# A transformer block on one core: the opening stage in another order

## The chip, the cores and the metric

The kernel runs on one core of a Trainium2 chip. The metric is device time in microseconds (us). A core has a matrix engine (PE), a vector engine (DVE), an engine for activations and copies (ACT), a general engine (POOL) and a queue engine (SP) that here only starts transfers. Each engine works through its own instructions in program order and waits on semaphores of the others.

## The reference

One pre-norm block for 2048 tokens of width 448. `x` is 2048x448, there are 16 heads of 28, one key and one value head for all of them, and a gated feed-forward part of width 1792.

```
q = (ln(x) @ wq).reshape(B, S, 16, 28).transpose(0, 2, 1, 3)
k, v = ln(x) @ wk, ln(x) @ wv
p = softmax(einsum("bhqd,bkd->bhqk", q, k) * 28 ** -0.5)
h = x + einsum("bhqk,bkd->bhqd", p, v) @ wo          # heads put side by side
out = h + (silu(ln(h) @ w1) * (ln(h) @ w3)) @ w2
```

## The kernel before, in words

**Numbers in two parts.** Every operand of a large product is split into a high part of reduced precision and a low part, the rest. A product takes the terms high-high, low-high and high-low. So whoever makes an operand makes two: ACT copies the high part (`xh`, `WQ[0]`, `WKV[0]`), DVE or POOL subtracts it (`xl` on DVE, `WQ[1]` and `WKV[1]` on POOL).

**Quarters.** The tokens are worked in four quarters of 512 (`t` = 0 to 3), each a tile `X[t]` of 128x4x448, that is 896 KB. The trace calls all four X, the order of instructions calls them X_77 to X_80. The heads are worked in four groups (`g`).

**The opening stage** (lines 389 to 575) makes keys and values for all quarters and the queries `QR[t][:, g]`. In it, for each quarter, stand these steps:

- `stats(t)`: on DVE four statistics (L178, L179) and one addition (L183), then on POOL a power that gives the reciprocal deviation `rs` (L184).
- `norm(t)`: four scalings of `X[t]` into `xn` on DVE (L189), each followed by a small copy on POOL (L191).
- `tr(t)`: sixteen transposes on PE (L203) into four banks of the matrix memory, four copies `xh` on ACT (L211), four subtractions `xl` on DVE (L221, L223).
- `kv(t)`: eleven matmuls on PE (L150). ACT copies the keys (L473) and values (L475), SP starts a transfer that doubles the keys (L476), and after each second quarter POOL forms the difference `kd` of two quarters' keys (L478). `k_low(t)` subtracts on DVE (L483).
- `va(t)`: four small transposes of the values (L490) and a copy on DVE (L491).
- `q(t, g)`: eleven matmuls on PE (L150, operand OS, which is `WQ`) and a copy of the result by ACT (L502). For the first one, `build_qs(0)` makes the split query instead (L238 on ACT, L239 on DVE); `build_qs(1)` and `build_qs(2)` do this from `QR`.

**Units.** Between them stand quads, which find the largest score of each row for the softmax. They go in pairs. The first quad of a pair is four matmuls against `kd` (L257) and four `relu` copies on ACT (L267); the second is four matmuls against the keys (L257) and four operations on DVE (L271, called "both" here) that add the `relu` to the score and take the maximum. The `relu` copies of the next pair go into the same buffers, so they wait for "both" of this pair. Q1 to Q20 are the quads in the order in which they come; odd ones are against `kd`.

**Banks.** There are eight banks. `bank()` takes the one that was given back longest ago in program order, `done()` gives one back. A matmul into a bank waits for the reader of what stood there. So the order of the code alone fixes which reader each step of PE waits for.

**Transfers.** Each transfer started by SP or ACT signals on one of eight semaphores (lanes) that are dealt out in turn. A transfer on a lane is started only when the transfer before it on that lane has landed. Until then the engine that is to start it waits, with all that stands behind it in its queue. At the start these transfers come: `X[0]` in four pieces, the small weights of keys and values (`wkv`: three transfers for `wk`, three for `wv`, all started by ACT), `WQ` (three transfers into OT: 672, 112 and 112 KB), and `X[1]` to `X[3]`.

**Behind the opening stage** comes the attention loop (lines 629 to 663), whose first score matmul (L308) stands directly behind the last `q`, and then the feed-forward part. PE goes through all of it in one fixed order.

Of the kernel before, what the change touches and what calls it, by code (L numbers as in the profile page):

```python
# [40 lines left out]
def block_kernel(  # L41
# [13 lines left out]
    ve, se, ge, pe, sy = nc.vector, nc.scalar, nc.gpsimd, nc.tensor, nc.sync  # L55
    xv = x[0].rearrange("(t p n) d -> t p n d", t=NT, p=P, n=NQ)
# [3 lines left out]
    def f(ap):  # L60
        return ap.bitcast(F32)
# [4 lines left out]
    ln_pool = ctx.enter_context(tc.tile_pool(name="ln", bufs=2))  # L66
# [68 lines left out]
    def done(ps):  # L135
        free.append(used.pop(id(ps))[1])
# [2 lines left out]

    def mm_D(ps, lhs, rhs, lsl, rsl, between=None, part=False):


        terms = []
        for a, b in ((0, 0), (1, 0), (0, 1)):
            terms += [(a, c, b, c) for c in range(3)]
        terms += [(0, 3, 0, 3), (0, 3, 1, 3)][: 2 - part]
        for k, (a, ca, b, cb) in enumerate(terms):
            pe.matmul(  # L150
                ps, lhs[b][:, cb, lsl], rhs[a][:, ca, rsl],
                start=(k == 0), stop=(k == len(terms) - 1 and not part),
            )
            if between is not None and k == 5:
                between()

    def load_w(dst, w, eng=sy):
        eng.dma_start(dst[:, 0:3], w[0:384].rearrange("(c p) m -> p c m", p=P))
        eng.dma_start(dst[0:64, 3], w[384:448])
        eng.dma_start(dst[64:128, 3], w[384:448])  # L160
# [9 lines left out]
    LN = {}  # L170

    def ln_stats(t, n):
        if n == 0:
            LN[t] = (ln_pool.tile([P, NQ, 6], F32, name="st", bufs=NT),
                     ln_pool.tile([P, NQ, 2], F32, name="mv", bufs=NT),
                     ln_pool.tile([P, NQ], F32, name="rs", bufs=NT), {})
        st, mv, _, _ = LN[t]
        ve.bn_stats(st[:, n], X[t][:, n])  # L178
        ve.bn_aggr(mv[:, n], st[:, n])  # L179

    def ln_rstd(t, n0=0, n1=NQ):
        _, mv, rs, _ = LN[t]
        ve.tensor_scalar(rs[:, n0:n1], mv[:, n0:n1, 1], EPS, None, op0=ALU.add)  # L183
        ge.tensor_tensor(rs[:, n0:n1], rs[:, n0:n1], pexp[:, n0:n1], op=ALU.pow)  # L184

    def ln_norm(t, n, spare=False):
        _, mv, rs, xns = LN[t]
        xn = xns[n] = ln_pool.tile([P, 512], F32, name="xn", bufs=4)
        (ge if spare else ve).tensor_scalar(xn[:, :D], X[t][:, n], mv[:, n, 0:1], rs[:, n : n + 1],  # L189
                                            op0=ALU.subtract, op1=ALU.mult)  # L190
# [208 lines left out]
    def wkv(tl, k):  # L399
        return tl[:, k, :384].rearrange("p (c m) -> p c m", c=4)  # L400
# [2 lines left out]
    wkv_r, WKV = wkv(slot(7, F32, "wkv"), 0), slot(6, F32R, "wkvs")  # L403
    WKV = [wkv(WKV, k) for k in range(2)]
    ve.memset(wkv_r, 0.0)
    for m0, w in ((0, wk), (64, wv)):
        load_w(wkv_r[:, :, m0 : m0 + DH], w, se)
    load_w(wq_r, wq)
    for t in range(1, NT):
        sy.dma_start(X[t], xv[t])  # L410
    kb = keep.tile([64, 1], F32, name="kb")
    ge.tensor_tensor(kb, ident[:64, 28:29], ident[:64, 60:61], op=ALU.add)
    for k in range(2):
        ve.memset(f(WQ[k][:, :, :, DH:]), 0.0)
    se.activation(NGT[0][:, :P // 4], ident[:, :P // 4], AF.Copy)
    warm = bank()

    def heat(n):
        for _ in range(n):
            pe.transpose(warm[:, :P], ident, ident)  # L420
# [14 lines left out]
    def low_wq(c0, c1, eng):  # L435
        for c in range(c0, c1 + 1):
            eng.tensor_tensor(WQ[1][:, c, :, :DH], wq4[:, c], f(WQ[0][:, c, :, :DH]), op=ALU.subtract)

    def split_wq(c0, c1, eng=None):
        for c in range(c0, c1 + 1):  # L440
            se.activation(WQ[0][:, c, :, :DH], wq4[:, c], AF.Copy)
            if eng:
                low_wq(c, c, eng)
# [11 lines left out]
    def stats(t, *ns):  # L455
        for n in ns:
            ln_stats(t, n)
        if NQ - 1 in ns:
            ln_rstd(t)

    def norm(t):
        for n in range(NQ):
            ln_norm(t, n)

    def tr(t, *cs):
        for c in cs or range(4):
            ln_tr(t, c)
# [13 lines left out]
    def k_low(t, ps):  # L481
        cols = slice(t * T, (t + 1) * T)
        ve.scalar_tensor_tensor(KL[0:64, cols], ps[0:64], kb, f(KH[0:64, cols]), op0=ALU.add, op1=ALU.subtract)  # L483
        sy.dma_start(f(KL[64:128, cols]), f(KL[0:64, cols]))
        done(ps)

    def va(t, vt):
        ps = bank()
        for n in range(NQ):
            pe.transpose(ps[:, 32 * n : 32 * n + 32], vt[64:96, n * P : (n + 1) * P], ident[64:96, 64:96])  # L490
        ve.tensor_copy(VA[:, NQ * t : NQ * t + NQ, :DH],  # L491
                       ps[:, :P].rearrange("p (n r) -> p n r", n=NQ)[:, :, :DH])
        done(ps)

    def q(t, g, between=None):
        ps = bank()
        mm_D(ps, [w[:, :, 4 * g : 4 * g + 4].rearrange("p c h r -> p c (h r)") for w in WQ],
             XT[t], slice(0, P), slice(0, T), between)
        if t == g == 0:
            build_qs(0, ps)  # L500
        else:
            se.activation(QR[t][:, g], ps, AF.Copy)  # L502
        done(ps)
# [6 lines left out]
    def quads(n=1):  # L510
        while n > 0 and first:
            fn, *args = first.pop(0)
            fn(*args)
            n -= fn is quad
# [5 lines left out]
            ln_norm(0, n - 1)  # L520
    ln_norm(0, NQ - 1)
    split_wkv()
    split_wq(0, 3)
    ln_tr(0, 0, between=lambda: heat(8))
    done(warm)
    tr(0, 1, 2, 3)
    low_wq(0, 3, ge)
    v0, p0 = kv(0)
    stats(1, 0, 1, 2, 3)
    q(0, 0)  # L530
    k_low(0, p0)
    norm(1)
    q(0, 1)
    tr(1)
    v1, p1 = kv(1)
    stats(2, 0, 1, 2, 3)
    q(0, 2)
    k_low(1, p1)
    norm(2)
    q(0, 3)  # L540
    va(0, v0)
    va(1, v1)
    build_qs(1)
# [4 lines left out]
    stats(3, 0, 1, 2, 3)
    q(1, 0, quads)
    k_low(2, p2)  # L550
    norm(3)
    quads()
    q(1, 1, quads)
    va(2, v2)
    quads()
    q(1, 2, quads)
    q(1, 3)
    build_qs(2)
    quads()
    tr(3)  # L560
    quads()
    v3, p3 = kv(3)
    load_wo()
    q(2, 0)
# [15 lines left out]
    def at(s, fn, *args):  # L580
        todo.setdefault(s, []).append((fn, args))
# [8 lines left out]
    LAST = NC * NI  # L590
# [9 lines left out]
            at(e + 14 + 2 * n, ln_stats, t, n)  # L600
        at(e + 22, ln_rstd, t)
    for n in range(NQ):
        at(LAST - 24 + n, ln_norm, 0, n, True)
    for c in range(4):
        at(LAST - 17.5 + 4 * c, lambda c: ln_tr(0, c, True, True), c)
    for t in range(NT):
# [195 lines left out]
```

## Time and profile before

| | |
|---|---|
| median of 3 runs | 1195.22 us (1195.06 to 1196.54) |
| the profiled execution | 1196.01 us, span 1194.2 us |
| busy: PE, DVE, ACT, POOL | 1178.6, 811.2, 724.0, 332.4 us |
| mean granted clock of PE | 0.998 |
| opening stage, up to the first score matmul | 92.75 us of the span |

The span is the time from the first to the last instruction on the core; all times below count from its start. A row of the timeline has the start, the time from the first start to the last end of the merged instructions, the engine, the line, the operation, what it writes and reads, how many there are, and in brackets how long the engine sat idle before it and what ended that. ACTq and SPq are the queue sides of ACT and SP that start transfers. Successive instructions of one engine overlap a little, so what a step costs in a row of equal ones is read from start to start.

### The profile page before, as it was taken

The numbers are of one execution on the slowest core, as the hardware profiler recorded it, in microseconds if no ns is written. First come the engines' busy times: TensorE is split into PE (matmuls) and PEld (weight loads), VectorE is DVE, ScalarE is ACT, GpSimd is POOL, SyncE is SP. The second block draws the span as 40 slices with busy tenths as digits, with TensorE's granted clock in tenths as the row PEclk, the third lists the DMA queues.
The fourth block names the chain that finished last, engine by engine and source line by source line (L and its number), as shares of the span: only waits on it lengthen the run. The fifth ranks groups of instructions, "written<-read, shape, count | busy, mean of one in ns | idle before, by whom it ended". The sixth has DMA issues, their size and how long they took to land. (4 is left out here: it accounts for less than half of the span.)

```text
span 1194.2 us, 24111 instructions
## 1 busy us (share of the span) xinstructions
PE 1178.6 (99%) x9594; PEld 728.6 (61%) x9594; DVE 811.2 (68%) x1486; ACT 724.0 (61%) x1377; POOL 332.4 (28%) x256
## 2 busy tenths in 40 slices
PE   8999999999999999999999999999999999999998
PEld 6664444445544445444445443688888888888886
DVE  6758999998899997899997982254444445444333
ACT  3568999997799996899996999411211111111111
POOL 4211011101101110110110132363555455445552
PEclk9999999999999999999999999999999999999999
DMA  5010001000001000010000010114000000000000
GB/s 167 19 37 2 27 10 46 11 12 2 11 4 44 12 12 2 11 47 5 8 12 10 2 46 11 40 45 117 1 32 1 1 1 31 1 1 32 1 1 32
DMA packets 32377, 26.92 MB, mean 23 GB/s; under 512 B 10824, under 2 KB 28936, under 8 KB 32264
## 3 DMA queue, kind: packets, MB, share of 16 engines
q1 hardware_dynamic: 31144, 25.27, 7.2%
q8 instruction: 75, 1.23, 0.4%
q14 instruction: 38, 0.31, 0.1%
q10 hardware_dynamic: 1120, 0.12, 0.1%
HBM read 20.25 MB, written 3.80 MB: 20 GB/s over the span
## 5 line engine op out<-in xcount | busy, mean ns | idle before, releaser
L318 ACT ACTIVATE pt<-pb 128x512 f32<-128x512 f32 x1024 | 531.5, 613 | 11.5 <-PE pb L308 5.5
L263 DVE TENSOR_REDUCE mx<-pa 128x1 f32<-128x512 f32 x708 | 460.7, 684 | 53.4 <-PE pb L308 38.1
L308 PE MATMUL pb<-qs,KH 32*128 32x512 f32 x2048 | 343.1, 431 | 0.1
L257 PE MATMUL pa<-KH,qs 32*128 32x512 f32 x866 | 326.6, 487 | 0.0
L326 PE MATMUL po<-pt,VA 128*32 128x256 f32 (+1 forms) x2984 | 298.2, 471 | 5.6 <-ACT OT L330 5.2
L308 PE MATMUL pb<-qs,KL 32*128 32x512 f32 x1024 | 284.6, 419 | 0.0
L308 PEld LDWEIGHTS pb<-qs,KH 32*128 32x128 f32 x2048 | 174.9, 183 | 113.9 <-DVE mx L263 50.1
L150 PE MATMUL pa<-xh,w 128*128 128x512 f32 x784 | 202.2, 391 | 0.0
L694 ACT ACTIVATE rb<-pa 128x512 f32<-128x512 f32 x56 | 30.4, 596 | 251.9 <-PE pa L686 251.9
L150 PEld LDWEIGHTS pa<-xh,w 128*128 128x128 f32 x784 | 146.2, 188 | 30.3 <-issue 1.2
L257 PEld LDWEIGHTS pa<-KH,qs 32*128 32x128 f32 x866 | 142.5, 182 | 9.5 <-issue 2.2
L711 PE MATMUL pb<-w2s,hid 128*128 128x448 f32 x672 | 145.0, 371 | 0.8 <-POOL w2s L380 0.8
L308 PEld LDWEIGHTS pb<-qs,KL 32*128 32x128 f32 x1024 | 136.6, 182 | 2.4
L711 PEld LDWEIGHTS pb<-w2s,hid 128*128 128x128 f32 x672 | 123.9, 188 | 21.5 <-issue 10.0
L326 PEld LDWEIGHTS po<-pt,VA 128*32 128x32 f32 x2984 | 59.1, 108 | 122.6 <-issue 105.3
L267 ACT ACTIVATE relu<-pa 128x512 f32<-128x512 f32 x158 | 91.7, 600 | 54.9 <-PE pa L257 38.6
L271 DVE CUSTOM_DVE_ANT_0 relu<-pa,relu 128x512 f32<-128x512 f32 x158 | 105.5, 682 | 11.3 <-ACT relu L267 9.7
L372 POOL TENSOR_TENSOR w<-QR,w 128x1024 fp32r<-128x1024 f32 x32 | 83.9, 2636 | 95.0 <-PE pa L686 81.4
L703 DVE TENSOR_TENSOR hid<-rb,hid 128x512 fp32r<-128x512 f32 x56 | 72.1, 1287 | 39.2 <-ACT hid L702 39.2
L350 POOL TENSOR_TENSOR OT<-OT,rb 128x512 f32<-128x512 f32 x16 | 20.5, 1283 | 273.9 <-ACT pt L318 102.8
L150 PE MATMUL pa<-xl,w 128*128 128x512 f32 x336 | 94.5, 390 | 0.0
L371 DVE CAST w<-QR 128x1024 fp32r<-128x1024 f32 x32 | 22.2, 694 | 90.5 <-PE pa L150 82.3
(96 smaller groups left out, 955.5 us busy)
## 6 DMA issues: line engine op xcount, KB each, us to landing
rb<-sd SPq DMA_DIRECT2D x64, 64.0 KB
QR<-in_B_w_dram SPq DMA_DIRECT2D x16, 192.0 KB
X<-in_A_x_dram SPq DMA_DIRECT2D x3, 896.0 KB
out_dram<-X SPq DMA_DIRECT2D x3, 896.0 KB
w<-in_B_w_dram SPq DMA_DIRECT2D x8, 192.0 KB
w_wo<-in_B_w_dram SPq DMA_DIRECT2D x6, 224.0 KB
qs<-ngt SPq DMA_DIRECT2D x64, 2.0 KB
sm<-OT SPq DMA_DIRECT2D x64, 2.0 KB
```

The costliest lines, as they stand in the source:

```text
L150: pe.matmul(ps, lhs[b][:, cb, lsl], rhs[a][:, ca, rsl], start=(k == 0), stop=(k == len(terms) - 1 and not part),)
L257: pe.matmul(self.ps, QS[i][r, 0, n * P : (n + 1) * P], ks[r], start=True, stop=True)
L263: ve.tensor_reduce(self.col(), self.ps, axis=AX.X, op=ALU.max)
L267: se.activation(r, self.ps, AF.Relu)
L271: ve.tensor_tensor_reduce(r, self.ps, r, 1.0, LOW, op0=ALU.add, op1=ALU.max, accum_out=self.col())
L308: pe.matmul(self.ps, (KH, KH, KL)[k][r, c * P : (c + 1) * P], QS[i][r, (0, 1, 0)[k]], start=(k == 0), stop=(k == 2))
L318: se.activation(pt, self.ps, AF.Exp, bias=0.0, scale=SCALE)
L326: pe.matmul(PO[i][32 * j : 32 * j + 32, q], VA[:, c], PT[i, c, j][:, q], start=(c == 0 and h0 == 0), stop=(c == NC - 1 and h1 == 2))
L372: ge.tensor_tensor(wl, W13[k], f(wh), op=ALU.subtract)
L694: se.activation(sg, ps[0], AF.Silu)
L703: ve.tensor_tensor(h[:, 1], sg, f(h[:, 0]), op=ALU.subtract)
L711: pe.matmul(Y[t][n][:, :D], hid[a][:, n * P : (n + 1) * P], w2s[:, b, :D], start=(k == 0 and m == 0), stop=(k == NF - 1 and m == 2))
```

## The change

Seven things are moved or replaced, all in the opening stage.

1. On SP, `X[1]` is loaded ahead of `WQ`.
2. On ACT, the first activation (it brings the table load with it) stands ahead of the six `wkv` transfers and reads `pexp`, not `ident`.
3. On ACT, the high parts of `WQ` stand behind the four `xh` copies of quarter 0.
4. On DVE, `norm(1)` stands directly behind `stats(1)`, ahead of the subtraction of `build_qs(0)` and of `k_low(0)`.
5. `norm(2)` and `norm(3)` are done by ACT: a scaling with a bias for each row. The bias `nb` is made by two more POOL instructions behind the power of `stats(2)` and `stats(3)`.
6. In every `q`, the fourth high-high term stands ahead of the low parts of `WQ`, so that these come last.
7. The quads are spread otherwise: `q(1, 0)` with Q2 inside it and Q3 stand ahead of `tr(2)`; a quad between `q(1, 2)` and `q(1, 3)` is new, the two around `tr(3)` are put together ahead of it.

```diff
     def mm_D(...):
+        if lows_last:
+            terms.insert(6, terms.pop(9))
...
     def ln_rstd(t, n0=0, n1=NQ, nbias=False):
...
+        if nbias:
+            ge.tensor_tensor(nb, mv[:, :, 0], rs, op=ALU.mult)
+            ge.tensor_scalar(nb, nb, -1.0, None, op0=ALU.mult)
...
+    def ln_norm(t, n, eng=ve):
...
+        if eng is se:
+            se.activation(xn[:, :D], X[t][:, n], AF.Identity, bias=nb[:, n : n + 1], scale=rs[:, n : n + 1])
+        else:
+            eng.tensor_scalar(xn[:, :D], X[t][:, n], mv[:, n, 0:1], rs[:, n : n + 1],
+                              op0=ALU.subtract, op1=ALU.mult)
...
+    se.activation(NGT[0], pexp[:, :1].to_broadcast([P, 32]), AF.Copy)
     for m0, w in ((0, wk), (64, wv)):
         load_w(wkv_r[:, :, m0 : m0 + DH], w, se)
+    sy.dma_start(X[1], xv[1])
     load_w(wq_r, wq)
-    for t in range(1, NT):
+    for t in range(2, NT):
...
-    split_wq(0, 3)
     ln_tr(0, 0, between=lambda: heat(8))
     done(warm)
     tr(0, 1, 2, 3)
+    split_wq(0, 3)
     low_wq(0, 3, ge)
     v0, p0 = kv(0)
-    stats(1, 0, 1, 2, 3)
+    stats(1)
+    norm(1, ve)
     q(0, 0)
     k_low(0, p0)
-    norm(1)
     q(0, 1)
     tr(1)
     v1, p1 = kv(1)
-    stats(2, 0, 1, 2, 3)
+    stats(2, True)
     q(0, 2)
+    norm(2, se)
+    q(0, 3)
     k_low(1, p1)
-    norm(2)
-    q(0, 3)
     va(0, v0)
     va(1, v1)
     build_qs(1)
     quads()
+    q(1, 0, quads)
+    quads()
     tr(2)
-    quads()
     v2, p2 = kv(2, quads)
```

The head of ACT's queue, before, with what each instruction waits for. DMAHW0 to DMAHW7 are the lanes; wkv and wkvs are the small weights as loaded and in two parts, OS_103 is `WQ[0]` and OT is `WQ` as loaded.

```order
L158 DMA wkv<-in_A_wk_dram 128x3x28 [waits DVE_49]
L159 DMA wkv<-in_A_wk_dram 64x28
L160 DMA wkv<-in_A_wk_dram 64x28
L158 DMA wkv<-in_A_wv_dram 128x3x28
L159 DMA wkv<-in_A_wv_dram 64x28 [waits DMAHW0_49]
L160 DMA wkv<-in_A_wv_dram 64x28 [waits DMAHW2_49]
L415 ACT_TABLE_LOAD
L415 ACTIVATE ngt_83<-ident 128x32 [waits Pool_49]
L429 ACTIVATE wkv<-wkv 128x4x28 [waits DMAHW5_49,DMAHW3_49,DMAHW1_49]
L430 ACTIVATE wkvs<-wkv 128x384 [waits DMAHW2_49,DMAHW6_49,DMAHW0_49,Activation_49]
L441 ACTIVATE OS_103<-OT 128x16x28 [waits DMAHW1_49]
```

The same place now. Lanes 0 to 3 are those of `X[0]`'s four pieces (its statistics wait for them), lane 4 is that of `X[1]`, lanes 5, 6 and 7 are those of `WQ`'s three transfers.

```order
L415 ACT_TABLE_LOAD
L415 ACTIVATE ngt_83<-pexp 128x32 [waits Pool_49]
L160 DMA wkv<-in_A_wk_dram 128x3x28 [waits DMAHW0_49,DVE_49]
L161 DMA wkv<-in_A_wk_dram 64x28 [waits DMAHW2_49]
L162 DMA wkv<-in_A_wk_dram 64x28 [waits DMAHW3_49]
L160 DMA wkv<-in_A_wv_dram 128x3x28 [waits DMAHW4_49]
L161 DMA wkv<-in_A_wv_dram 64x28 [waits DMAHW5_49]
L162 DMA wkv<-in_A_wv_dram 64x28 [waits DMAHW6_49]
L439 ACTIVATE wkv<-wkv 128x4x28 [waits DMAHW3_49,DMAHW2_49,DMAHW0_49]
L440 ACTIVATE wkvs<-wkv 128x384 [waits DMAHW5_49,DMAHW6_49,DMAHW4_49,Activation_49]
L220 ACTIVATE xh<-pb 128x512 [waits PE_49] x4
```

The six small transfers, which took lanes in between `X[0]`'s, now come behind eight of SP's transfers, and the last three wait for `X[1]` and two of `WQ`'s; the `xh` copies of quarter 0 moved ahead of OS_103 and stand directly behind them.

ACT's queue from the keys of quarter 1 on, before. QR_96 holds the queries of quarter 0 and QR_97 those of quarter 1; pb and pa are banks.

```order
L473 ACTIVATE KH<-pb,kb 64x512
L475 ACTIVATE vt<-pb 32x512
L502 ACTIVATE QR_96<-pb 128x512 x2
L238 ACTIVATE qs<-QR_96 128x512
L267 ACTIVATE relu<-pa 128x512 x2
L267 ACTIVATE relu_117<-pa 128x512 x2
L211 ACTIVATE xh<-pb 128x512 x4
```

And now:

```order
L482 ACTIVATE KH<-pb,kb 64x512
L484 ACTIVATE vt<-pb 32x512
L511 ACTIVATE QR_96<-pb 128x512
L196 ACTIVATE xn<-X_79,nb,rs 128x448 x4
L511 ACTIVATE QR_96<-pb 128x512
L247 ACTIVATE qs<-QR_96 128x512
L276 ACTIVATE relu<-pa 128x512 x2
L276 ACTIVATE relu_117<-pa 128x512 x2
L511 ACTIVATE QR_97<-pb 128x512
```

The four scalings of quarter 2 stand between the copies of `q(0, 2)` and `q(0, 3)`, ahead of the `relu` copies of Q1; the `xh` copies of quarter 2 moved behind a second set of `relu` copies.

PE's queue from the values' transposes on, before (203 are transposes of `xn`, 257 with kd and KH the quads):

```order
L490 MATMUL pb<-ident,vt 128x32 x8
L257 MATMUL pa<-kd,qs 128x512 x4
L203 MATMUL pb<-ident,xn 128x128 x16
L257 MATMUL pa<-KH,qs 128x512 x4
L150 MATMUL pb<-xh,wkvs 96x512 x3
L150 MATMUL pb<-xl,wkvs 96x512 x3
L257 MATMUL pa<-kd,qs 128x512 x4
L150 MATMUL pb<-xh,wkvs 96x512 x5
```

And now:

```order
L499 MATMUL pb<-ident,vt 128x32 x8
L266 MATMUL pa<-kd,qs 128x512 x4
L152 MATMUL pb<-xh,OS_103 128x512 x3
L152 MATMUL pb<-xl,OS_103 128x512 x3
L266 MATMUL pa<-KH,qs 128x512 x4
L152 MATMUL pb<-xh,OS_103 128x512
L152 MATMUL pb<-xh,OS_104 128x512 x4
L266 MATMUL pa<-kd,qs 128x512 x4
L212 MATMUL pb<-ident,xn 128x128 x16
```

`q(1, 0)` now stands where the transposes of quarter 2 stood. Its bank is the one that `q(0, 3)` filled.

More of the change, by code (lines that the diff above doesn't have):

```diff
@@ L136, in done, with mm_D @@
         free.append(used.pop(id(ps))[1])
-    def mm_D(ps, lhs, rhs, lsl, rsl, between=None, part=False):
+    def mm_D(ps, lhs, rhs, lsl, rsl, between=None, part=False, lows_last=False):
         terms = []
@@ L414, in block_kernel @@
         ve.memset(f(WQ[k][:, :, :, DH:]), 0.0)
-    se.activation(NGT[0][:, :P // 4], ident[:, :P // 4], AF.Copy)
     warm = bank()
@@ L453, in split_wo, with stats, norm @@
         ge.tensor_tensor(WO[1][:, g], wo_r[:, g], f(WO[0][:, g]), op=ALU.subtract)
-    def stats(t, *ns):
-        for n in ns:
+    def stats(t, nbias=False):
+        for n in range(NQ):
             ln_stats(t, n)
-        if NQ - 1 in ns:
-            ln_rstd(t)
-    def norm(t):
+        ln_rstd(t, nbias=nbias)
+    def norm(t, eng):
         for n in range(NQ):
-            ln_norm(t, n)
+            ln_norm(t, n, eng)
     def tr(t, *cs):
@@ L497, in q @@
         mm_D(ps, [w[:, :, 4 * g : 4 * g + 4].rearrange("p c h r -> p c (h r)") for w in WQ],
-             XT[t], slice(0, P), slice(0, T), between)
+             XT[t], slice(0, P), slice(0, T), between, lows_last=True)
         if t == g == 0:
@@ L544, in block_kernel @@
     quads()
+    q(1, 0, quads)
+    quads()
     tr(2)
-    quads()
     v2, p2 = kv(2, quads)
[L548 to L551, printed above, removed]
+    stats(3, True)
     quads()
     q(1, 1, quads)
+    norm(3, se)
+    k_low(2, p2)
     va(2, v2)
@@ L556, in block_kernel @@
     q(1, 2, quads)
+    quads()
     q(1, 3)
@@ L560, in block_kernel @@
     tr(3)
-    quads()
     v3, p3 = kv(3)
@@ L602, in block_kernel @@
     for n in range(NQ):
-        at(LAST - 24 + n, ln_norm, 0, n, True)
+        at(LAST - 24 + n, ln_norm, 0, n, ge)
     for c in range(4):
```

14 lines of the change are left out of this document (6 added, 8 removed).

## The prediction

> **What bounds the kernel now.** First the busy times, then the order of PE's work up to the attention loop.
>
> ```profile
> PE 1178.6 (99%) x9594; PEld 728.6 (61%) x9594; DVE 811.2 (68%) x1486; ACT 724.0 (61%) x1377; POOL 332.4 (28%) x256
> ```
>
> PE is the bound, and it has one fixed order. What the opening stage gains or loses on PE, the whole kernel gains or loses, since nothing behind it is changed. So only the stage is read, from PE's timeline:
>
> ```profile
> 12.41 1.45 PE L150 MATMUL pb<-xh,wkvs 128*96 128x512 f32 x3 [1.24 <-ACT xh L211]
> ...
> 22.66 2.82 PE L203 MATMUL pb<-ident,xn 128*128 128x128 f32 x16
> ...
> 28.25 0.86 PE L150 MATMUL pb<-xh,OS 128*128 128x512 f32 x3
> 28.95 0.86 PE L150 MATMUL pb<-xl,OS 128*128 128x512 f32 x3
> ...
> 34.47 2.82 PE L203 MATMUL pb<-ident,xn 128*128 128x128 f32 x16
> ...
> 40.57 0.49 PE L257 MATMUL pa<-kd,qs 32*128 32x512 f32 x1 [0.23 <-DVE mx L271]
> ...
> 58.17 0.51 PE L257 MATMUL pa<-kd,qs 32*128 32x512 f32 x4
> 58.60 1.97 PE L203 MATMUL pb<-ident,xn 128*128 128x128 f32 x16
> 60.50 1.38 PE L257 MATMUL pa<-KH,qs 32*128 32x512 f32 x4
> ...
> 65.28 0.86 PE L150 MATMUL pb<-xh,OS 128*128 128x512 f32 x3
> ...
> 92.75 0.50 PE L308 MATMUL pb<-qs,KH 32*128 32x512 f32 x1
> ```
>
> I cut the stage in three: up to 28.25, where kv(1) is done; from there to 65.28, where kv(3) is done; and the rest to 92.75, whose steps the change leaves in their places. From start to start three matmuls take 0.70 (28.25 to 28.95), so eleven take 2.57; a quad takes 0.43, sixteen transposes 1.90 when nothing holds them. The middle part holds 6.22 up to 34.47, and then four q (10.3), two kv (5.1), two sets of transposes (3.8), nine quads (3.9) and va(2) (I put 0.4): 29.7. It lasts 37.03, so 7.3 us of it are holes. That is all that spreading can win there.
>
> **The change, first part: when the small weights land.** SP and the two queues' rows:
>
> ```profile
> 0.72 1.82 SPq L393 DMA_DIRECT2D X<-in_A_x_dram  x4
> 5.06 0.39 SPq L158 DMA_DIRECT2D OT<-in_A_wq_dram  x1
> ...
> SPq L158 <- DMA wkv<-in_A_wk_dram: 2.5, 1, 2.5
> ```
>
> ```profile
> 1.28 0.44 ACTq L158 DMA_DIRECT2D wkv<-in_A_wk_dram  x1
> ...
> 4.14 0.61 ACTq L160 DMA_DIRECT2D wkv<-in_A_wv_dram  x1
> ...
> 6.60 0.52 ACT L430 ACTIVATE wkvs<-wkv 128x384 fp32r<-128x384 f32 x1
> 9.90 1.98 ACT L441 ACTIVATE OS<-OT 128x448 fp32r<-128x448 f32 x4 [2.78 <-DMA OT<-in_A_wq_dram]
> 11.79 2.04 ACT L211 ACTIVATE xh<-pb 128x512 fp32r<-128x512 f32 x4
> ...
> 33.59 0.60 ACT L502 ACTIVATE QR<-pb 128x512 f32<-128x512 f32 x1 [1.97 <-PE pb L150]
> 34.08 0.62 ACT L238 ACTIVATE qs<-QR 128x512 fp32r<-128x512 f32 x1
> 34.60 2.05 ACT L267 ACTIVATE relu<-pa 128x512 f32<-128x512 f32 x4
> ```
>
> SP stood 2.5 us for a lane that a wkv transfer held: the wait for a lane is real. Now it turns round. SP has no such wait and starts X[0], X[1] and WQ in one go; the last wkv transfer waits on ACT until WQ's second transfer has landed. Ahead of that lie 896 + 896 + 672 + 112 KB. DVE's timeline has the first landing, at 3.39, and the durations used further down:
>
> ```profile
> 3.39 0.63 DVE L178 BATCH_NORM_STATS2 st<-X 128x6 f32<-128x448 f32 x1 [1.01 <-DMA X<-in_A_x_dram]
> ...
> 20.75 0.69 DVE L239 TENSOR_TENSOR qs<-pb,qs 128x512 fp32r<-128x512 f32 x1 [2.49 <-ACT qs L238]
> 21.36 0.73 DVE L483 SCALAR_TENSOR_TENSOR KL<-pb,kb,KH 64x512 fp32r<-64x512 f32 x1
> 22.02 1.76 DVE L189 TENSOR_SCALAR xn<-X,mv,rs 128x448 f32<-128x448 f32 x4
> 24.83 1.89 DVE L221 TENSOR_TENSOR xl<-pb,xh 128x512 fp32r<-128x512 f32 x3 [1.05 <-ACT xh L211]
> ...
> 41.04 0.69 DVE L271 CUSTOM_DVE_ANT_0 relu<-pa,relu 128x512 f32<-128x512 f32 x1
> ...
> 41.65 0.69 DVE L271 CUSTOM_DVE_ANT_0 relu<-pa,relu 128x512 f32<-128x512 f32 x1
> ...
> 42.26 0.62 DVE L178 BATCH_NORM_STATS2 st<-X 128x6 f32<-128x448 f32 x1
> ...
> 45.44 0.69 DVE L271 CUSTOM_DVE_ANT_0 relu<-pa,relu 128x512 f32<-128x512 f32 x1
> ```
>
> Three stretches of 5 us; the last column is GB/s, the third from the end the granted clock:
>
> ```profile
> 5.00:10.00 5.00, 4.84 (x44) 4.48 (x42) 3.84 (x12) 2.10 (x5) 3.39 (x9) 1.00 0.88 228
> 10.00:15.00 5.00, 3.73 (x18) 2.15 (x17) 2.58 (x4) 3.82 (x8) 5.00 (x5) 0.97 1.01 407
> 15.00:20.00 5.00, 5.00 (x17) 3.75 (x16) 3.06 (x10) 1.27 (x2) 1.23 (x2) 0.69 0.39 138
> ```
>
> The first 224 KB landed at 3.39; the other 2352 KB (2.41 MB) take 5.9 us at the 407 of the full stretch, so they land at 9.3 at the earliest; I allow up to 10.5. From the start of the last wkv transfer to its use passed 6.60 - 4.14 = 2.46. So the small weights are there between 11.8 and 13.0, against 6.60 now, if nothing is in their way. X[2] and X[3] are on the same way then (896 KB at 407 is 2.25 us each): at worst 15.2. I take L = 13.4, since the first wkv transfer, started at 1.28 beside X[0], landed only at 5.06, 1.3 us slower than the last.
>
> The Trainium skill, "DMA: Bandwidth & Descriptors", section "Queues, rings and completion order", says that each engine of the transfers changes between the queues only after a whole packet of descriptors, so a small transfer waits for what the other queue has in hand. By that rule L would lie in the later half of this range; the trace agrees so far as those 1.3 us go.
>
> What hangs on L is a chain of ACT, POOL and DVE, worked with these rows of POOL and those above:
>
> ```profile
> 1.38 0.18 POOL L412 TENSOR_TENSOR kb<-ident 64x1 f32<-64x1 f32 x1
> ...
> 10.77 4.45 POOL L437 TENSOR_TENSOR OS<-OT,OS 128x448 fp32r<-128x448 f32 x4
> 18.34 1.02 POOL L184 TENSOR_TENSOR rs<-rs,pexp 128x4 f32<-128x4 f32 x1 [3.12 <-DVE rs L183]
> ...
> 31.51 1.29 POOL L478 TENSOR_TENSOR kd<-KH 128x512 fp32r<-128x512 f32 x1 [7.27 <-DMA KH<-KH]
> 32.76 1.02 POOL L184 TENSOR_TENSOR rs<-rs,pexp 128x4 f32<-128x4 f32 x1
> ```
>
> L430's copy 0.5, the four xh 2.0, WQ's first high part 0.55 (a quarter of 1.98 and its own latency), WQ's low parts 4.45, the power 1.02 (it stands behind them on POOL), norm(1) 1.76, then build_qs(0) and k_low(0) 1.27 (20.75 to 22.02): xl of quarter 1 starts at L + 11.55. It starts at 24.83 now. The break-even is L = 13.3. So kv(1), which xl feeds, ends at 28.25 + 0.1. That X[1] is there early gives nothing: its statistics stand behind the xl of quarter 0 on DVE. kv(0) starts some 2 us later than 12.41, but q(0, 0) has to wait for WQ's last low part at L + 7.5 = 20.9 anyway; with lows last its other seven matmuls are done by then, so it ends at 21.2, q(0, 1) at 23.8, and tr(1) takes 1.9 where it now takes until xn is there. First part: +0.1, from -1.5 (L 11.8) to +1.9 (L 15.2).
>
> **Second part, from the end of kv(1), called E.** PE is ready for q(1, 0) at E + 6.22. Its bank is read by the copy of q(0, 3), which stands on ACT behind the four scalings of quarter 2. These wait for nb, which stands on POOL behind kd (E + 3.26, held by the keys' transfer), the power (to E + 5.53) and two instructions that no row shows. The nearest row is kb's 0.18, the far end the power's 1.02; I take 0.5 for both, because their size is that of kb and not a power, with bounds of 0.36 and 2.04. The scalings I price by L441's 1.98 for four of the same size. E + 6.0, + 8.0, the copy 0.6: q(1, 0) starts at E + 8.6, a hole of 2.4. Queued behind on ACT are build_qs(1) and the relu copies of Q1 (now at E + 6.35, then at E + 8.95).
>
> From there, by readers of banks: Q2 at 10.0, "both" (0.61 each, 41.04 to 41.65) to 13.0, tr(2) 12.3 to 14.2, the relu copies of Q3 to 14.5 and only then xh: kv(2) starts at 15.1, paced by xl, and ends at 18.9. Q6 waits for the relu copies of Q5 until 21.4. Its "both" stand behind stats(3), 3.2 us on DVE (42.26 to 45.44), and end at 25.9; Q7 and q(1, 2) wait for them, 2.7 us. Q8 waits for Q7's relu copies, which stand behind the scalings of quarter 3 on ACT, to 27.5. q(1, 3) starts at 29.8, tr(3) ends at 34.7, and xl of quarter 3 stands behind the "both" of Q10, so kv(3) ends at E + 38.4. Before it is E + 37.0. What the change wins there (0.85 at tr(2), 34.47 against 1.90; the hole up to 40.57; 1.7 behind 60.50) it gives back at q(1, 0), Q7 and kv(3). Second part: +1.4; with nb at its bounds +1.3 to +2.9, and -0.3 if each hand-over is 0.15 shorter than I put it in about a dozen. The price of the last term order is nothing: the same eleven matmuls, with WQ ready.
>
> **Third part.** 0: same steps, same banks' spacing, PE without holes.
>
> **Sum:** +0.1 + 1.4 = +1.5. The profiled execution's span of 1194.2 becomes 1195.7, its 1196.01 becomes 1197.5. It lies 0.8 above the median of 1195.22, so for the median I say **1196.7**.
>
> **The rivals.** A difference of 0.2% (2.4 us: below 1192.8, above 1197.6) is about what a measurement of this kernel can tell from no change.
>
> *The clock (slower).* The granted clock was 0.69 in 15 to 20 and 0.97 in 10 to 15: 1.55 + 0.15 = 1.7 us lost, behind the stretch in which PE waited for xh. After the change PE waits longer there (11.2 to 14.5) and again from E + 6.2 to E + 8.6. If one more such loss falls where POOL does not cover it, it adds 1.7: 1198.4. It decides when PE stands for over 2 us in one piece. For: both waits are longer than the 1.24 that preceded the loss. Against: the holes in the middle part cost no clock now. Chance 0.17.
>
> The Trainium skill, "TensorE: Matmul & The Clock Gate", section "What's actually happening", says that the clock halves after an idle window of about 3.4 us and that these windows run freely. By that rule one halved window costs 1.7 us, which agrees with the trace, and whether a wait of 2.4 us brings one depends on where the window lies.
>
> *The small weights stay behind X[2] and X[3].* L = 15.2 adds 1.8: 1198.5. For: SP's queue no longer pauses. Chance 0.13.
>
> *The lanes do not hold the small weights.* Then they are there before the xh copies; these run from 9.9 to 11.9, WQ's low parts end at 12.45 + 4.45 = 16.9, xl(1) starts at 21.0, 3.8 earlier. With +1.4 that is -2.4: 1192.8. Against it speaks SP's wait. Chance 0.12.
>
> **How the numbers follow.** Forecast 0.5, its own range 1195.4 to 1198.0; the rivals 0.17, 0.13, 0.12; 0.08 for what I have not seen, half of it on either side. Above 1197.6 lie nearly all of the first two, 0.05 of the forecast and part of the rest: 0.34. Below 1192.8 half of the third and some of the rest: 0.1. Range 1193.2 to 1199.4.
>
> **What would show it.** Right: L440 starts on ACT near 13.4 and the wait before it is for a transfer; kv(0) starts on PE near 14.5; the copy of q(0, 3) ends 8.6 behind kv(1) and PE stands 2.4 us before q(1, 0); 38.4 from kv(1) to kv(3); the first score matmul near 94.2. Wrong: L440 before 10, or no wait at q(1, 0), or a second stretch of low clock.

## The result and the profile after

The changed kernel takes 1212.99 us (median of 4 runs, 1212.14 to 1213.48) against 1195.38 for the kernel before beside it: ratio 1.0145 [1.0127, 1.0162], slower by 17.6 us. The forecast was 1196.7, its range ended at 1199.4. The profiled execution's span is 1210.8, 16.6 above that of before.

PE's timeline of the changed kernel at the places that the prediction named (start, time, engine, line, what it writes and reads, how many, the idle time before and what ended it):

```profile
17.88 1.71 PE L152 MATMUL pb<-xh,wkvs 128*96 128x512 f32 x3 [6.23 <-ACT xh L220]
...
32.97 0.86 PE L152 MATMUL pb<-xh,OS 128*128 128x512 f32 x3
...
42.40 1.65 PE L152 MATMUL pb<-xh,OS 128*128 128x512 f32 x3 [3.21 <-ACT QR L511]
...
51.16 1.45 PE L152 MATMUL pb<-xh,wkvs 128*96 128x512 f32 x3 [0.80 <-ACT xh L220]
...
76.17 0.86 PE L152 MATMUL pb<-xh,OS 128*128 128x512 f32 x3
...
103.58 0.49 PE L317 MATMUL pb<-qs,KH 32*128 32x512 f32 x1
...
768.03 0.96 PE L152 MATMUL pa<-xh,w 128*128 128x512 f32 x3
769.52 1.80 PE L152 MATMUL pa<-xh,w 128*128 128x512 f32 x7
771.16 0.86 PE L152 MATMUL pa<-xl,w 128*128 128x512 f32 x3
```

And the feed-forward part of before, which the prediction did not read:

```profile
757.38 0.97 PE L150 MATMUL pa<-xh,w 128*128 128x512 f32 x3
...
761.17 1.75 PE L150 MATMUL pa<-xh,w 128*128 128x512 f32 x7
762.75 0.84 PE L150 MATMUL pa<-xl,w 128*128 128x512 f32 x3
```

| stretch | before | after | difference |
|---|---|---|---|
| start to the end of kv(1) | 28.25 | 32.97 | +4.7 |
| end of kv(1) to the end of kv(3) | 37.03 | 43.20 | +6.2 |
| from there to the first score matmul | 27.47 | 27.41 | -0.1 |
| attention, to the first feed-forward matmul | 664.63 | 664.45 | -0.2 |
| feed-forward part, to the end | 436.8 | 442.8 | +5.9 |

So three places lose, and one of them stands in work that the change does not touch. There seven matmuls take 1.64 us from start to start (769.52 to 771.16) where they took 1.58 (761.17 to 762.75).

ACT's timeline after, with its transfers (ACTq), shows the first two:

```profile
0.72 1.28 ACT L415 ACT_TABLE_LOAD   x1 [0.72 <-PEq L797]
...
3.33 0.44 ACTq L160 DMA_DIRECT2D wkv<-in_A_wk_dram  x1
...
12.94 0.47 ACTq L161 DMA_DIRECT2D wkv<-in_A_wv_dram  x1
13.67 0.49 ACTq L162 DMA_DIRECT2D wkv<-in_A_wv_dram  x1
...
16.82 0.52 ACT L440 ACTIVATE wkvs<-wkv 128x384 fp32r<-128x384 f32 x1 [2.24 <-DMA wkv<-in_A_wv_dram]
...
39.15 2.71 ACT L196 ACTIVATE xn<-X,nb,rs 128x448 f32<-128x448 f32 x4 [2.82 <-POOL nb L190]
41.77 0.57 ACT L511 ACTIVATE QR<-pb 128x512 f32<-128x512 f32 x1
```

The last two `wkv` transfers wait for `WQ`'s first two, which have landed by 12.94 and 13.67, and the small weights are copied at L = 16.82 (13.4 was forecast). The four scalings take 2.62 up to the next copy, and q(1, 0) starts behind a hole of 3.21.

The windows after (busy times of PE, PEld, DVE, ACT and POOL, then the granted clock, the share of the transfer engines, GB/s):

```profile
5.00:10.00 5.00, 5.00 (x42) 5.00 (x41) 3.73 (x12) 0.00 (x0) 3.09 (x8) 1.00 0.99 342
10.00:15.00 5.00, 1.64 (x16) 1.40 (x13) 0.00 (x0) 0.30 (x1) 0.00 (x0) 1.00 0.87 239
15.00:20.00 5.00, 2.12 (x5) 1.32 (x6) 2.11 (x4) 3.18 (x7) 1.17 (x2) 0.66 0.58 186
20.00:25.00 5.00, 5.00 (x17) 3.59 (x16) 4.13 (x10) 2.42 (x5) 4.89 (x5) 0.66 0.02 5
40.00:45.00 5.00, 2.60 (x6) 1.82 (x6) 0.00 (x0) 4.80 (x9) 2.20 (x5) 0.55 0.00 0
45.00:50.00 5.00, 5.00 (x29) 3.44 (x29) 2.54 (x8) 1.94 (x5) 0.00 (x0) 0.77 0.01 2
```

A mean c over 5 us is 10(1 - c) us at half clock, if only full and half are granted: 3.4 + 3.4 from 15 to 25, and 4.5 + 2.3 from 40 to 50. That is 6.8 us twice, where before had 3.4 once. Windows of 1 us put them at 16.6 to 23.4 and at 40.5 to 47.3, so each begins in a hole of PE, of 6.2 and of 3.2 us.

### The profile page after: what moved, and what is told of

Same layout as the page of the kernel before. It is cut to its first block, busy times and chain, and to the rows that moved or that the text cites. A ratio compares the mean times of both kernels' runs of the same rounds, so it can differ in the third digit from the quotient of the medians.

```text
span 1210.8 us, 24122 instructions
## 1 busy us (share of the span) xinstructions
PE 1186.8 (98%) x9594; PEld 731.1 (60%) x9594; DVE 810.0 (67%) x1478; ACT 728.8 (60%) x1385; POOL 332.1 (27%) x260
## 5 line engine op out<-in xcount | busy, mean ns | idle before, releaser
L152 PE MATMUL pa<-xh,w 128*128 128x512 f32 x784 | 206.0, 396 | 0.0
```

The source lines that it names most:

```text
L152: pe.matmul(ps, lhs[b][:, cb, lsl], rhs[a][:, ca, rsl], start=(k == 0), stop=(k == len(terms) - 1 and not part),)
```

## The experiments

The theory before the runs had three parts. (1) The new tile `nb` (four times 32 bytes in each partition) lies in a pool in front of the big slots and moves them by 128 bytes, which makes the feed-forward matmuls slower. (2) The first activation ahead of the `wkv` transfers gives the lanes to SP's transfers, and L is late by that. (3) The hole before q(1, 0) costs more in clock than in waiting. Rivals: the feed-forward part is slow as a consequence of the other front; the small weights are late because of the amount that is loaded, not the lanes; the quads' new places cost the middle part, not the scalings on ACT.

**e1_shift: before, with the unused tile `nb` added.**

```diff
                      ln_pool.tile([P, NQ], F32, name="rs", bufs=NT), {},
+                     ln_pool.tile([P, NQ], F32, name="nb", bufs=NT))
```

> The kernel before, with four tiles of 32 bytes that nothing uses, in the place where the changed kernel has its bias nb. Every tile behind them (xn, rb, all slots with the split weights w and the hidden values) stands 128 bytes further on, as in the changed kernel; no instruction differs. Theory 'place': the feed-forward part loses 5.8 us in the changed kernel because its operands stand at other addresses; then this one takes 1195.4 + 5.8 = 1201, with the matmuls of L150 there at 232 ns from start to start, not 227, and the opening stage still ends at 92.75. Rival 'phase': the later start or another step of the change brings that loss; then this one takes 1195.4.

Measured: 1201.20 us, ratio 1.0049 [1.0032, 1.0066]; the span is 1200.2, and the feed-forward part (from 757.38, the same as before) takes 442.8. The two groups of its matmuls in before (busy time in us, mean ns of one; successive ones overlap, so one lasts longer than the step from start to start):

```profile
L150 PE MATMUL pa<-xh,w 128*128 128x512 f32 x784 | 202.2, 391 | 0.0
...
L150 PE MATMUL pa<-xl,w 128*128 128x512 f32 x336 | 94.5, 390 | 0.0
```

and in e1_shift:

```profile
L150 PE MATMUL pa<-xh,w 128*128 128x512 f32 x784 | 205.9, 396 | 0.0
...
L150 PE MATMUL pa<-xl,w 128*128 128x512 f32 x336 | 96.3, 395 | 0.0
```

What follows: an unused tile alone costs 6.0 us, with the old front. It is 5 ns in each of 784 + 336 matmuls, 5.6 us by these rows.

**e2_noshift: the changed kernel, with `nb` in a pool of its own behind the slots.**

```diff
+    nb_pool = ctx.enter_context(tc.tile_pool(name="nbs", bufs=2))
...
-                     ln_pool.tile([P, NQ], F32, name="nb", bufs=NT))
+                     nb_pool.tile([P, NQ], F32, name="nb", bufs=2))
```

> The changed kernel with nb in a pool of its own behind the slots, so that every other tile stands where it stood before; no instruction differs from the changed kernel. Theory 'place': 1213.0 - 5.8 = 1207.2, the opening stage still ends near 103.6. Rival 'phase': 1213.

Measured: 1208.28 us, ratio 1.0112 [1.0097, 1.0127]; the feed-forward part takes 436.8 again. What follows: the loss in the feed-forward part is one of place, shown from both sides. The front was worse in this profile than in the changed kernel's (L = 19.05, first score matmul at 106.69), with the same order: when the small transfers land differs by some us from one profile to the next. So it does in the order of before, with L = 6.60 in before and 9.46 in e1.

**e3_lanes: e2, with the first activation back behind the `wkv` transfers.**

```diff
-    se.activation(NGT[0], pexp[:, :1].to_broadcast([P, 32]), AF.Copy)
     for m0, w in ((0, wk), (64, wv)):
         load_w(wkv_r[:, :, m0 : m0 + DH], w, se)
...
+    se.activation(NGT[0][:, :P // 4], ident[:, :P // 4], AF.Copy)
```

> e2 with the first activation (and its table load) put back behind the six small transfers, on ident as before. The small transfers then take their lanes in between X[0]'s again and wait for nothing of X[1] or WQ. Theory 'lanes': the copy of the small weights starts near 7 instead of 16.8, kv(0) on PE near 11 instead of 17.9, kv(1) ends 5 us or more ahead of the changed kernel's 33.0, and the time falls by 5 to 8 us against e2. Rival 'WQ late': the order X[1] ahead of WQ alone makes q(0, 0) late; then kv(0) is early but kv(1) ends within 2 us of 33.0.

Measured: 1201.05 us, ratio 1.0052 [1.0037, 1.0067]. ACT's timeline of e3:

```profile
1.28 0.43 ACTq L161 DMA_DIRECT2D wkv<-in_A_wk_dram  x1
...
4.13 0.61 ACTq L163 DMA_DIRECT2D wkv<-in_A_wv_dram  x1
...
9.80 0.53 ACT L441 ACTIVATE wkvs<-wkv 128x384 fp32r<-128x384 f32 x1 [3.32 <-DMA wkv<-in_A_wv_dram]
```

All six small transfers start by 4.13, with the same bytes on the way. L is 9.80 (near 7 was expected), kv(1) ends at 24.99, and no clock is lost up to there. So the place of this one instruction makes L late and is worth 7.2 us; that it works through the lanes is read from the rows of the changed kernel, where each of the six transfers starts behind the landing that it is to wait for. The hole before q(1, 0) is still there (3.23), and so is the clock behind it; e3's windows:

```profile
30.00:35.00 5.00, 1.77 (x15) 1.18 (x14) 0.52 (x2) 3.81 (x7) 1.94 (x8) 0.81 0.00 1
35.00:40.00 5.00, 5.00 (x15) 3.10 (x13) 1.76 (x5) 1.84 (x4) 1.26 (x1) 0.50 0.01 2
```

**e4_dve: e2, with norm(2) and norm(3) on DVE, without `nb`; the quads stay in their new places.**

```diff
-    stats(2, True)
+    stats(2)
...
-    norm(2, se)
+    norm(2, ve)
```

and the same for quarter 3.

> e2 with norm(2) and norm(3) on DVE in their new places in the program, without the two POOL instructions for nb. Theory 'hole': the 3.2 us in which PE waits before q(1, 0), and the 6.8 us of half clock that begin there, come from the scalings standing on ACT ahead of the copy of q(0, 3). Then the hole goes, the second stretch of half clock with it, and the stretch from kv(1) to kv(3) shrinks from 43.2 to 38 or less: 5 us or more below e2. Rival: DVE is then late instead, with the transposes of quarter 2 or Q2, and the stretch stays over 41.

Measured: 1203.16 us, ratio 1.0070 [1.0055, 1.0085]. PE's timeline of e4 at q(1, 0):

```profile
37.74 0.48 PE L267 MATMUL pa<-kd,qs 32*128 32x512 f32 x1
38.15 0.96 PE L153 MATMUL pb<-xh,OS 128*128 128x512 f32 x3
```

PE goes on without a wait, with no loss of clock there, and kv(3) ends 39.07 behind kv(1), 3.4 us at half clock (from 56.3) included. So the scalings on ACT make the hole, not the quads' places. The half clock from 56.3 has no such hole ahead of it:

```profile
54.78 1.74 PE L267 MATMUL pa<-kd,qs 32*128 32x512 f32 x3 [0.29 <-DVE mx L281]
56.61 1.65 PE L153 MATMUL pb<-xh,OS 128*128 128x512 f32 x3
```

In the 5 us before it the longest wait that PE's rows name is 0.29. What brings this stretch is not shown.

**e5_both: e3 and e4 together.**

> e3 and e4 together: X[1] ahead of WQ, WQ's split behind the xh copies, norm(1) early, WQ's low parts last, and the quads in their new places, but the small weights' transfers as before and all scalings on DVE. If the two repairs add up, kv(1) ends near 25 (e3: 25.0), the stretch to kv(3) is 36 to 39 (e4: 39.1, with 3.4 us at half clock in it), the opening stage ends near 89 to 91.5 and the time is 2 to 4 us below before. Rival: DVE is late instead in the middle part when it comes earlier; then the stretch is over 40 and the time that of before.

Measured: 1196.87 us (10 runs), ratio 1.0009 [1.0001, 1.0018]; L = 10.33, kv(3) 38.96 behind kv(1), again with 3.4 us at half clock (from 50.8). The 2 to 4 us below before that were expected did not come. What follows: with the three causes undone the 17.6 us are gone but for 1. What is left of the change gains 1.6 up to kv(1) (26.69) and loses 1.9 in the middle part.

**e6_first: only the first part of the change** (`X[1]` ahead of `WQ`, `WQ`'s high parts behind `xh`, norm(1) early, low parts last); first activation, norms and quads as before.

```diff
+    sy.dma_start(X[1], xv[1])
     load_w(wq_r, wq)
...
-    split_wq(0, 3)
     ln_tr(0, 0, between=lambda: heat(8))
     done(warm)
     tr(0, 1, 2, 3)
+    split_wq(0, 3)
...
+    norm(1, ve)
     q(0, 0)
     k_low(0, p0)
-    norm(1)
```

> The first part of the change alone, without the move of the table load: X[1] ahead of WQ, WQ's split behind the xh copies, norm(1) early, WQ's low parts last; from stats(2) on the order and the engines of before. Theory 'two parts': kv(1) ends near 25 instead of 28.25, the stretch to kv(3) is 37.0 as before, the opening stage ends near 89.5 and the time is 3 us below before (1192). Rival 'given back': the middle part is held by transfers and by POOL's kd, so it grows by what the first part wins; 1195.

Measured: 1194.39 us (12 runs, 1192.41 to 1195.78) against 1195.72, ratio 0.9983 [0.9975, 0.9992]. PE's timeline of e6:

```profile
26.74 0.86 PE L153 MATMUL pb<-xh,OS 128*128 128x512 f32 x3
...
63.75 0.86 PE L153 MATMUL pb<-xh,OS 128*128 128x512 f32 x3
...
91.22 0.50 PE L318 MATMUL pb<-qs,KH 32*128 32x512 f32 x1
```

kv(1) ends 1.5 earlier than before, the middle part is as before (37.01), and no clock is lost in front. This is the one version that beats the kernel before, by 1.3 us, where 3 were expected. ACT's timeline shows what holds it:

```profile
13.93 1.98 ACT L452 ACTIVATE OS<-OT 128x448 fp32r<-128x448 f32 x4 [1.11 <-DMA OT<-in_A_wq_dram]
```

The `xh` copies are done, and ACT waits 1.11 for `WQ`, which now lands behind `X[1]`; in e3's profile, with the same order up to here, it did not wait (12.14).

**e7_middle: only the middle part** (quads and norms as in the change, `nb` behind the slots); all up to kv(1) as before except the last term order.

> The middle part of the change alone: quads in their new places and norm(2) and norm(3) on ACT, with nb behind the slots; everything up to kv(1) as before. Theory 'two parts': kv(1) ends near 28.3, the stretch to kv(3) is 43 to 45, of it some 3 us by half clock, and the time is 6 to 8 us above before (1201 to 1203). My prediction's working, which leaves the clock out, has 38.4 for the stretch: 1196.6.

Measured: 1201.11 us, ratio 1.0044 [1.0031, 1.0057]; the middle part takes 42.50, with a hole of 3.22 before q(1, 0) and 3.4 us at half clock behind it. So the middle part loses 5.5 by itself, whatever stands in front. In the change it loses 6.2, with 6.8 us at half clock.

**e8_warm: e3, with 24 transposes of `ident` on PE ahead of q(1, 0).** Their results are not used.

```diff
+    for _ in range(24):
+        pe.transpose(va1[:, P : 2 * P], ident, ident)
```

> e3 with 24 transposes of the identity on PE between Q1 and q(1, 0), into a bank that is free there; their results are not used. They fill the 3.2 us in which PE waits for the copy of q(0, 3). Theory 'clock': the stretch of half clock from 33.1 to 39.9 in e3 comes from that idle time; then it goes, q(1, 0) with Q2 in it takes 3.2 us instead of 5.8, and the opening stage ends 2 to 3 us earlier than in e3 (95.9), although PE has more to do. Rival: the half clock is set by something else; then it stays, the transposes take twice as long and the stage ends later than in e3.

Measured: 1198.88 us (6 runs), ratio 1.0025 [1.0014, 1.0036]. e8's windows:

```profile
30.00:35.00 5.00, 4.92 (x41) 3.87 (x40) 0.52 (x2) 2.93 (x5) 2.72 (x8) 1.00 0.11 26
35.00:40.00 5.00, 4.68 (x27) 3.14 (x27) 2.43 (x7) 3.90 (x9) 1.37 (x2) 1.00 0.00 2
```

and its PE timeline:

```profile
25.88 0.86 PE L153 MATMUL pb<-xh,OS 128*128 128x512 f32 x3
...
35.32 0.96 PE L153 MATMUL pb<-xh,OS 128*128 128x512 f32 x3 [0.34 <-ACT QR L514]
...
41.92 1.46 PE L153 MATMUL pb<-xh,wkvs 128*96 128x512 f32 x3 [0.67 <-ACT xh L221]
...
46.44 0.97 PE L153 MATMUL pb<-xh,OS 128*128 128x512 f32 x3
...
66.94 0.86 PE L153 MATMUL pb<-xh,OS 128*128 128x512 f32 x3
```

With PE busy in the hole the clock stays at 1.00 and the middle part takes 41.06, not e3's 43.47, though q(1, 0) still waits for the same copy. So of the middle part's 6.2 us some 2.4 are clock, shown by taking the clock's cause away and leaving the wait. The other profiles with the change's middle part agree: it grows with the time at half clock in it.

| half clock in the middle part, us | middle part, us |
|---|---|
| 0 | 41.06 (e8) |
| 3.4 | 42.50 (e7), 42.50 (e10, below) |
| 6.8 | 43.20 (after), 43.47 (e3) |
| 10.2 | 44.96 (e2), 44.99 (e9, below) |

All but e8 have a hole of 3.18 to 3.23 before q(1, 0), and half clock begins in it or at most 1.2 behind it. The last 6.8 us of e2 and e9 come later (from 64.5 and 59.7), at the place where e4 has its stretch and, like that, with no wait over 0.3 just ahead.

The Trainium skill, "TensorE: Matmul & The Clock Gate", section "What's actually happening", says that the half clock follows an idle window of about 3.4 us, that it ends after a busy one, and that these windows run freely. The stretches of 3.4 and 6.8 us agree with that unit, and so does it that work without use in the hole keeps the clock. But holes of 3.21 and 3.23, shorter than the stated idle window, brought a stretch too, and e4's came with no wait over 0.3 just ahead, so here the measurement decides. The prediction took it from that rule that a wait of 2.4 us may bring a stretch, by where the window lies. By the page's words it would not: 2.4 us of idle time cannot fill a window of 3.4.

**p1_all64, p2_slots128, p3_all256: e6, with tiles without use ahead of the slots**, one run each, beside a before of 1195.08. p1 moves the slots, and the LayerNorm tiles ahead of them, by 64 bytes; p2 the slots alone by 128; p3 both by 256.

```diff
+    pad = ln_pool.tile([P, 16], F32, name="pad", bufs=1)
```

(p1; in p3 64 for 16; in p2 a pool of its own with 32, directly ahead of the slots.)

> e6 with 64 unused bytes at the head of the pool of the statistics, so that everything behind (xn, rb, the slots) stands 64 bytes further on. e6's feed-forward part lasts 437.0 us, that of the changed kernel and of e1 (128 bytes) 442.7 and 442.8. If the place matters by steps of 128 bytes or by what shares an address with the left operands, 64 may give either of the two, or something between: there is no theory on it yet.

> e6 with 128 unused bytes directly ahead of the slots: only the slots (split weights w, hidden values) move, while xn and rb stay. Theory 'slots': the matmuls of the feed-forward part read their weights from the moved slots, so it lasts 442.8. Rival 'rb or xn': 437.0.

> e6 with 256 unused bytes at the head of the pool of the statistics. If the loss grows with the distance: 448 for the feed-forward part; if it comes with one place and goes with the next: 437; if any move does it: 443.

Measured: feed-forward parts of 441.7, 442.7 and 436.9; the times are 1200.9, 1197.9 and 1194.96. It is the slots' place alone (p2), and not the amount that they move: 64 and 128 bytes slow the matmuls, 256 do not. In before the tiles in between add up so that the slots (with `w`) begin 45824 bytes behind `xh`, which is 179 x 256. So either that distance counts or the slots' own address.

**p4_pair128 and p5_xh128** tell these apart, one run each beside 1194.96. p4 moves `xh` and the slots by 128 bytes, so the distance stays; p5 moves `xh` by 128 and the slots by 256.

```diff
+    pad = xt_pool.tile([P, 32], F32, name="pad", bufs=1)
...
+    gap = ctx.enter_context(tc.tile_pool(name="gap", bufs=1))
+    pad2 = gap.tile([P, 32], F32, name="pad2")
```

(p4 has the first line alone.)

> As e6_first, with 128 bytes without use ahead of xh, so that xh and the slots both move by 128 bytes and their distance stays 45824. If the distance of the two operands counts: the feed-forward part takes 437 and the two groups of its matmuls 391 and 390 ns. If the slots' own address counts (a multiple of 256 off its place in before): 442 to 443 us and 395 to 396 ns, as in p2_slots128.

> As e6_first, with 128 bytes ahead of xh and 128 more directly ahead of the slots: xh moves by 128, the slots by 256, their distance grows by 128. If the distance counts: 442 to 443 us and 395 to 396 ns. If the slots' own address counts: 437 us and 391 ns, as in p3_all256.

Measured: feed-forward parts of 437.4 and 442.0, times of 1195.81 and 1199.17. The groups of p4:

```profile
L154 PE MATMUL pa<-xh,w 128*128 128x512 f32 x784 | 202.3, 391 | 0.0
...
L154 PE MATMUL pa<-xl,w 128*128 128x512 f32 x336 | 94.6, 390 | 0.0
```

and of p5:

```profile
L156 PE MATMUL pa<-xh,w 128*128 128x512 f32 x784 | 205.9, 396 | 0.0
...
L156 PE MATMUL pa<-xl,w 128*128 128x512 f32 x336 | 96.3, 395 | 0.0
```

The distance between the two operands counts. At 0 and 256 bytes beyond the 45824 the matmuls have their old pace, at 64 and 128 they lose 5 ns. The slots' own address does not: in p4 they move by 128 and nothing is lost, in p5 by 256 and the loss is there. The tiles between `xh` and the slots move with `xh` in p4 and p5; that the distance is the one to `xh` and `xl` is taken from these being the slowed matmuls' other operand. Why the distance matters is open.

**e9_alone: e2, with `X[2]` and `X[3]` loaded only behind the keys' transfer.**

```diff
-    for t in range(2, NT):
-        sy.dma_start(X[t], xv[t])
...
     v0, p0 = kv(0)
+    for t in range(2, NT):
+        sy.dma_start(X[t], xv[t])
```

> e2 with X[2] and X[3] loaded behind the keys' transfer of quarter 0, so that nothing is on the way beside X[0], X[1], WQ and the small weights. (The last small transfer then waits for WQ's first transfer, not the second: some 0.7 us less.) Theory 'beside X': L, the start of the copy of the small weights, was 16.8 in the changed kernel and 19.1 in e2 because X[2] and X[3] run beside WQ's last rows and the small transfers; then WQ's first transfer lands near 10 instead of 12.9, the small weights 2.5 after the last issue instead of 3.2 to 4.1, and L is 12 to 13, as the prediction's sum has it without them. Rival: the small transfers themselves are slow behind any load; L stays over 15.

Measured: 1205.59 us (one run, beside 1195.08), L = 14.38, kv(1) at 29.58. ACT's timeline of e9:

```profile
12.41 0.47 ACTq L163 DMA_DIRECT2D wkv<-in_A_wv_dram  x1
...
14.38 0.52 ACT L439 ACTIVATE wkvs<-wkv 128x384 fp32r<-128x384 f32 x1 [0.80 <-DMA wkv<-in_A_wv_dram]
```

With 1792 KB less on the way L is earlier than in the changed kernel and in e2 (16.82, 19.05), but still not 13.4. Here the last small transfer waits only for `WQ`'s first, and this lands at 12.41, which is behind the 10.5 allowed for the second.

**e10_wqfirst: e9, with `X[1]` behind `WQ`.**

```diff
-    sy.dma_start(X[1], xv[1])
     load_w(wq_r, wq)
+    sy.dma_start(X[1], xv[1])
```

> As e9_alone, with X[1] loaded behind WQ instead of ahead of it; the last small transfer now waits for WQ's second transfer, and less lies ahead of that (X[0] and WQ: 1.68 MB behind the first 224 KB have to be in, not 2.41). If the amount ahead of the awaited transfer sets its landing: at 342 to 349 GB/s from 3.39 it lands near 8 to 8.5 and the small weights are copied near 10 to 11. If the end of WQ is slow by itself, whatever stands ahead: its landing stays behind 11 and the copy near 13 to 14.

Measured: 1203.28 us (one run, beside 1194.96), L = 14.01. ACT's timeline of e10:

```profile
10.77 0.60 ACTq L163 DMA_DIRECT2D wkv<-in_A_wv_dram  x1
...
14.01 0.52 ACT L439 ACTIVATE wkvs<-wkv 128x384 fp32r<-128x384 f32 x1 [0.93 <-DMA wkv<-in_A_wv_dram]
```

and its window from 5 to 10:

```profile
5.00:10.00 5.00, 5.00 (x42) 4.87 (x41) 3.83 (x11) 0.00 (x0) 2.86 (x7) 1.00 1.01 281
```

Neither side came as expected: `WQ`'s first transfer lands at 10.25 and its second has landed by 10.77, earlier than in the changed kernel (13.67) and later than the 8 to 8.5 of the amount, and then the small ones take 3.24 where 1.97 were enough in e9. The transfer engines are full from 5 to 10 (share 1.01) and yet move 281 GB/s. So less in the way helps to start the last small transfer, but L gains 0.4 of the 1.6 us. That `X[1]`, now behind `WQ` on SP's queue, takes the rest by sharing its end is likely and not shown apart. Only starting the small ones first (e3) brings L to 10. Why full engines move between 281 and 407 GB/s stays open.

## Why the prediction was wrong

**Step by step, what held.** The order of waits was as written: the last `wkv` transfer waits on ACT for `WQ`'s second, kv(0) for the small weights, q(1, 0) for the copy of q(0, 3) behind four scalings behind `nb`. From the first of the two `nb` instructions to the first scaling pass 0.57 us (38.58 to 39.15; 0.5 was taken). The chain from L to kv(1), "break-even 13.3", held to 0.3 in e2, e9 and e3: it gives +5.8, +1.1 and -3.5 for their L, and 6.0, 1.3 and -3.3 were measured. It did not hold where something else came later than it took: in e5 and e6 `WQ` itself, with kv(1) 1.4 behind the chain, and in the changed kernel PE (below).

**First part: the size of L failed.** "The other 2352 KB (2.41 MB) take 5.9 us at the 407 of the full stretch" put `WQ`'s second transfer at 9.3 to 10.5. It had landed only by 13.67, with 342 and 239 GB/s in the two stretches up to 15. The 407 was the fastest of its kind: other stretches from 10 to 15 with full engines moved 284 (p1) to 396 (e1). To that came 3.15 from the last start to the copy, where 2.46 had been measured in the other order. With L = 16.82 the chain gives +3.5. Of the other 1.2 of the 4.7, 0.9 is a wait that the chain did not have, in DVE's timeline after:

```profile
29.55 1.89 DVE L230 TENSOR_TENSOR xl<-pb,xh 128x512 fp32r<-128x512 f32 x3 [0.93 <-ACT xh L220]
```

Here `xl` of quarter 1 waits for PE's transposes, not for DVE. PE is late because kv(0) ran at half clock: it took 4.92 (17.88 to 22.80), in e3 at full clock 3.12. e2 and e9, where PE works some 3 us of this at half clock, have no such wait; e10, with 3.4, waits 0.41 and lies 0.6 over the chain, e4, with over 5, 1.0. A run that removes this clock alone was not made. The rival with L = 15.2 named part of the cause: without `X[2]` and `X[3]` (e9) L is 14.38, 2.4 less than in the changed kernel and still past 13.4, so its price of 1.8 was too small. The rival "lanes do not hold" had nearly the right price (-3.8) for what e3 then made true (-3.3 at kv(1)).

**Second part: the clock failed as a side case, and the middle was sized too short.** It was a rival at 0.17 with 1.7 for one loss. Both of its waits came, both longer than put (6.2, against 3.3 from 11.2 to 14.5, and 3.2 against 2.4), and each brought 6.8 us at half clock; in the middle that costs 2.4. "The holes in the middle part cost no clock now" was weak evidence, since the longest wait that PE's rows name there is 0.73 (at 62.61). Nor is "over 2 us in one piece" the condition: e4 lost clock with no wait over 0.3 just ahead, while in front a wait of 1.24 was followed by half clock in before and one of 1.37 in e7 was not. Without the clock (e8) the middle takes 41.06, not 38.4. Of those 2.7, 0.8 are there at q(1, 0) (35.32 is E + 9.4, against 8.6), 0.6 of them from scalings that start 0.65 apart where L441's copies gave 0.5. At the end of kv(2) it is 1.7 (20.6 against 18.9), at the end 2.7. The rest are hand-overs, put too short one by one and not taken apart further; the lower bound that took them shorter had the wrong sign.

**Third part: "same steps, same banks' spacing" failed.** The steps are the same, the operands' places are not: `nb` moved the slots by 128 bytes and with them `w`, +5.9 us. Nothing in the profile of before could size this, but that the change adds tiles in a pool ahead of the slots stood in the diff, and "nothing behind it is changed" was wrong by that alone.

**The sum as it came:** 3.5 + 1.2 (L and its clock), 1.4 as forecast for the middle + 2.7 beyond it (e8), 2.1 left for the middle's clock (2.4 between e3 and e8), 5.9 (place), -0.3 in the two stretches behind kv(3): 16.5 of 16.6. The range to 1199.4 holds e8 (1198.88), where the lanes, the middle's clock and the place are undone; with the place alone undone (e2, 1208.28) the forecast would have been wrong too.

## What to carry to other kernels

When a step moves on an engine that also starts transfers, list the order in which all queues take lanes and take the time of the last landing from the slowest row, not from the fullest stretch. Count a hole on PE of some 3 us as the hole and a half-clock stretch behind it (it came in all six profiles with one before q(1, 0), worth 1.3 us for each 3.4 by the table above), and see whether other PE work can lie in it. A new tile, however small, can move every tile behind it and so change the pace of matmuls far away: compare the addresses of their operands before and after, or put the tile last.

## What the runs showed of the hardware

- The pace of the feed-forward's 128x512 matmuls hangs on the distance in memory between their two operands: one lasts 389 to 391 ns (seven start within 1.58 us) at 179 x 256 bytes and at 256 more, 395 to 397 ns (1.64) at 64 or 128 more. The whole part went from 437 to 442 or 443 us. No other distances were tried.
- A hole of 3.2 us on PE was followed by 3.4 or 6.8 us at half clock (e7, e3); with 24 small transposes in it there was none (e8). A hole is not the only cause: a stretch also came with no wait over 0.3 just ahead (e4, e5, e2, e9).
- Six small transfers that started behind large ones were usable at 14.0 to 19.1 us; started first, at 6.6 to 10.5.
